# Attention with a Fourier-mixed FFN: the last block's fold in two parts, group 1's statistics and token sums later, the first streamed forms in h's place

## The chip, the cores and the metric

The kernel runs on one core of one Trainium2 chip. The metric is the device time of one execution in microseconds (us), as the median of several runs. The engines are TensorE (PE; PEld is its weight load), VectorE (DVE), ScalarE (ACT), GpSimd (POOL) and SyncE (SP), which issues nearly all DMAs.

## The reference

Attention over 4 batches, 8 heads, 768 tokens and head size 64, where a token sees 4 sink tokens and the 128 latest ones; then, over tokens (4, 768, 512), the real part of a two-dimensional FFT, a layer norm and a two-layer ReLU FFN:

```
x = attention(q, k, v)                         # (4, 768, 512)
u = x + real(fft(fft(x, axis=1), axis=2))
un = (u - mean(u)) / sqrt(var(u) + 1e-6)       # over the 512 channels
out = u + relu(un @ w_ch1) @ w_ch2             # 512 -> 2048 -> 512
```

All of it is float32. A product on PE is made of three: each factor is split in a high part that PE takes as it is and a low part (the rest), and hi·hi, hi·lo and lo·hi are added. So for each factor an engine casts the high part (ACT mostly) and another subtracts it (DVE or POOL).

## The kernel before

Tokens go in 24 blocks of 128, batches in the order 0, 2, 1, 3. Attention and the Fourier stage of the batch before it are interleaved in steps written out by hand; from step 97 on the tile scheduler orders the instructions of each engine by times of its own model and by pairs "this issues after that" (`issue_after`).

**Fourier stage of a batch.** `fold_n` (L355) adds and subtracts block j and block j + 3, `fold_m` (L362, L365) folds the 512 columns about their middle, `fold_hi` (L368, ACT) and `fold_lo` (L371, DVE) split the result into gh and gl. `stage1` (L398) multiplies by cosines and sines: za uses columns 0 to 255, zr column 256, zb the columns from 257 on. `stage2` gives a (L425) and b (L446), `combine` (L451, L452) their difference and sum d, `update` (L462, L463) adds d to u. The last batch to be folded is batch 3, whose third pair of blocks (j = 2) contains the last token block of attention. In the tail the updates of batch 2 run beside it.

**FFN.** The 24 blocks form six groups of four. Group 0 is computed directly: for each f = 0 to 15 (128 of the 2048 hidden units) `ch1` (L703, 12 matmuls, first layer), `split` (relu's high part on ACT L1192, low part on DVE L1193) and `ch2` (L1199, 12 matmuls, second layer) of the f before. Meanwhile the weights arrive as pairs of 32-bit words (raw) and are converted to float32 by `convert`: three DVE steps (L639 to L641), ACT's high part and POOL's low part, for the first layer into w_ring (L650, L651), for the second into w (L665, L666). W1's pairs of blocks are also combined for the later groups by `combine_w1` on POOL: four differences tq (L677 to L680), of which ACT and POOL make high and low parts `to` (L685, L686); SP stores w_ring and `to` in a DRAM tensor (L654, L687).

Groups 1 to 5 use seven products for each pair of halves in place of eight. The forms of W1 are streamed from that DRAM tensor into eight places (`load`, L1394, issued on SP) and used by `product` (L1421: 12 matmuls of 256 columns, PSUM banks pA, pB, pC). ACT and DVE put the products together, `halves` splits the relu into hring, and `unit` (L1449) is the second layer. The places are the buffers ld of the raw weights, `to`, tq and h. hring lies in the buffer of group 0's transposed tokens (un_slots), free after the last `ch1`. Tokens of the next group are prepared beside a group: statistics (L530 to L552), deviations, `make` (normalise), `turn` (transpose on PE into a PSUM bank, copied by ACT into xf, L1257), and sums of token halves (L1298, L1301) with their high (L1295) and low parts. For group 1 this is the generator `prepare_1`, of which three steps follow each f from 6 on.

Of the kernel before, what the change touches and what calls it, by code (L numbers as in the profile page):

```python
# [19 lines left out]
P = 128  # L20
# [42 lines left out]
F_LAST = (1, 1), (2, 2), (3, 3)  # L63
# [142 lines left out]
def kernel(  # L206
# [67 lines left out]
    def run(general):  # L274
        tag = "g" if general else ""
        with ExitStack() as p1:
# [59 lines left out]
            def fourier(b, at, ready):  # L336
# [20 lines left out]
                def fold_m(eng, j, odd):  # L357

                    g = t_["eo", j, 0]
                    if odd:  # L360
                        t = t_.pop(("eo", j, odd))
                        eng.tensor_tensor(g[:, 257:512], t[:, 1:256], t[:, 511:256:-1], op=ALU.subtract)  # L362
                        t_["g", j] = t_.pop(("eo", j, 0))
# [3 lines left out]
                def fold_hi(j):  # L367
                    A.copy(gh[:, j], t_["g", j])  # L368

                def fold_lo(j):  # L370
                    V.tensor_tensor(gl[:, j], t_.pop(("g", j)), f32(gh[:, j]), op=ALU.subtract)  # L371
# [97 lines left out]
                for j in range(NHALF):  # L469
# [3 lines left out]
                    f_n, f_m, f_s = F_LAST if tail and j == NHALF - 1 else (F_N, F_M, F_S)  # L473
# [153 lines left out]
            def convert(i, pool=None):  # L627
# [16 lines left out]
                if which == 0:  # L644
# [6 lines left out]
                    G.tensor_tensor(d[1], tf, f32(d[0]), op=ALU.subtract)  # L651
# [19 lines left out]
            def combine_w1(p, pool):  # L671

                t = state.pop(("t", p))
                b11, b21, b12, b22 = t[:, 0, :256], t[:, 0, 256:], t[:, 1, :256], t[:, 1, 256:]
# [516 lines left out]
            def split(h, x):  # L1191
                state["relu"] = A.activation(h[0], x, AF.Relu).ins  # L1192
                V.scalar_tensor_tensor(h[1], x, 0.0, f32(h[0]), op0=ALU.max, op1=ALU.subtract)  # L1193
# [144 lines left out]

            po = [ps_o.tile([P, DM], F32, tag=f"o{i}", name=f"o{i}_0") for i in range(len(groups[0]))]
            hs = {}  # L1340
            for i in (2, 3):
                convert(i, wa)
            for f in range(NF):
                ps = hp.pop(0) if f < 2 else ch1(0, f, unT0)
                hs[f] = g0.tile([P, 2, 512], F32R, tag="h", name=f"h_sb{f}", bufs=2)
                hs[f] = [hs[f][:, i] for i in range(2)]
                split(hs[f], ps)
                if pw is None:
# [21 lines left out]
                for _ in range(PREP_N if f >= PREP else 0):  # L1370
                    next(steps, None)
# [4 lines left out]
            for i in sorted(stores):  # L1376
                for fn in stores.pop(i):
                    fn()
# [3 lines left out]


            T_PLACE = {1: 0, 2: 1, 4: 2, 6: 3}
            stream = [(w_dram, it, W_PLACE[k]) for it in range(NIT) for k in range(7)]
            for g in range(2, len(groups)):
                stream += [(w_dram, i, W_PLACE[k]) for it in range(0, NIT, 2) for k in range(7) for i in (it, it + 1)]
                stream += [(t_dram, it, T_PLACE[k]) for k in (1, 2, 4) for it in range(NIT)]

            def load(n):  # L1390
                if n < len(stream):
                    d, it, k = stream[n]
                    for j in range(2):
                        nc.sync.dma_start(f32(places[n % NWS][:, j]).rearrange("p s c -> p (s c)"), d[2 * it + j][:, k])  # L1394

            w1_t = g0.tile([P, 2, 2, 2, 256], F32R, tag="to", name="w1_t")
            places += [w1_t[:, 0], w1_t[:, 1], g0.tile([P, 2, 2, 256], F32R, tag="tq", name="w1_q")]
            places.append(g0.tile([P, 2, 2, 256], F32R, tag="h", name="w1_h0", bufs=2))
            for n in range(NWS - 1):
                load(n)  # L1400
# [4 lines left out]
            with tc.manual_schedule():  # L1405
# [3 lines left out]
                hring = npool.tile([P, 4, 2, 2, 256], F32R, tag="un_slots", name="hring", bufs=1)  # L1409
# [4 lines left out]
                def product(n, k, ps):  # L1414
                    w = places[n % NWS]
# [8 lines left out]
                    load(n + NWS)  # L1424
# [75 lines left out]
                load(NWS - 1)  # L1500
# [292 lines left out]
```

## Time and profile before

| | |
|---|---|
| runs, us | 746.4, 746.86, 748.05; median 746.86 |
| the profiled execution | 747.63; span 745.9, so 1.73 around it |
| mean granted clock of PE | 0.994 |
| busy, us | PE 715.6, DVE 560.5, ACT 357.3, POOL 274.4 |
| first FFN group, end of the attention | about 210 to 326.7 us of the span |
| group 1 | 326.7 to 416.5 us |

Times in the timelines are from the start of the span. A timeline's row gives the start, the length of a run of like instructions, the engine, the line, what is written and read, the shape, the count, and in brackets how long the engine stood before it and what ended that. In the list of waits each row has the total, the number of waits and the longest.

### The profile page before, as it was taken

To read this page: it belongs to the slowest core of one execution; us is meant where nothing else is said; L and a number is where in the kernel's file an instruction comes from. 1 tells how busy PE (TensorE), PEld (TensorE's weight loads), DVE (VectorE), ACT (ScalarE), POOL (GpSimd) and SP (SyncE) were. 2 spreads that over 40 slices of the span, in tenths; PEclk is the share of its full clock that TensorE was granted. 3 is DMA by queue.
4 is the path that set the end of the run, shared out by engine and by line. 5 is a ranking of instruction groups with operands and counts; after the bars stand their busy time and mean duration, and the time that the engine had idled before them with its cause. 6 is when DMAs were issued, how large, how long until landed. Compare 5 with 4: busy or idle time off the path is not lost.

```text
span 745.9 us, 15695 instructions
## 1 busy us (share of the span) xinstructions
PE 715.6 (96%) x5539; PEld 642.6 (86%) x5539; DVE 560.5 (75%) x1299; ACT 357.3 (48%) x901; POOL 274.4 (37%) x391
## 2 busy tenths in 40 slices
PE   8999998989979999898999999999999999999996
PEld 6776876867868888687989999999999999999996
DVE  7778578888899988858668667947697578846773
ACT  5887666766634537313324134534444245523541
POOL 3567467577557989824994000000000000000000
PEclk9999999999999999999999999999999999999998
DMA  9863525533207999779999798979974897759721
GB/s 304 289 173 106 149 73 165 174 94 103 86 21 237 328 346 330 277 277 385 374 301 327 246 348 277 313 239 379 375 242 167 321 378 261 255 205 390 269 98 62
DMA packets 109576, 181.69 MB, mean 244 GB/s; under 512 B 9868, under 2 KB 44812, under 8 KB 108336
## 3 DMA queue, kind: packets, MB, share of 16 engines
q1 hardware_dynamic: 109200, 176.83, 69.6%
q0 software_dynamic: 288, 3.76, 1.3%
q8 instruction: 46, 0.75, 0.4%
q14 instruction: 42, 0.34, 0.1%
HBM read 148.04 MB, written 32.51 MB: 242 GB/s over the span
## 4 chain that ended last, share of the span: by engine, by line
PE 50%; DVE 4%; ACT 1%; issue 1%; SPq 0%; DMA 0%; POOL 0%; DVEq 0%
PE pB L1421 10%; PE qB L1598 9%; PE pA L1421 7%; PE pC L1421 6%; PE qC L1598 6%; PE qA L1598 6%; PE o L1449 5%; DVE bn L530 1%; PE unt L571 1%; DVE hring L1193 0%; DVE x L1657 0%; DVE x L1660 0%; SPq L1394 0%; DVE un L565 0%; DVE stat L531 0%
## 5 line engine op out<-in xcount | busy, mean ns | idle before, releaser
L1620 ACT CAST hring<-x 128x512 fp32r<-128x512 f32 x92 | 57.0, 619 | 52.0 <-PE qB L1598 19.6
L811 ACT ACTIVATE sm<-sm,mx 128x132 f32<-128x132 f32 x192 | 75.9, 400 | 4.6 <-DVE mx L805 4.6
L1624 DVE TENSOR_TENSOR hring<-x,hring 128x512 fp32r<-128x512 f32 x92 | 63.4, 689 | 14.8 <-ACT hring L1620 9.3
L786 PE MATMUL s<-ring,q 64*128 64x260 f32 x320 | 49.0, 411 | 5.9 <-DVE mx L805 2.7
L805 DVE CUSTOM_DVE_ANT_0 sm<-s,mask 128x132 f32<-128x132 f32 x192 | 48.5, 293 | 6.2 <-DVE s L792 0.9
L703 PE MATMUL h<-un_slots,w_ring 128*128 128x512 f32 x192 | 49.7, 405 | 3.4 <-POOL w_ring L651 2.9
L703 PEld LDWEIGHTS h<-un_slots,w_ring 128*128 128x128 f32 x192 | 36.3, 194 | 12.4 <-POOL w_ring L651 4.1
L786 PEld LDWEIGHTS s<-ring,q 64*128 64x128 f32 x320 | 26.9, 185 | 18.2 <-issue 5.0
L1598 PE MATMUL qA<-w,hring 128*128 128x256 f32 x312 | 39.8, 279 | 0.0
L1449 PE MATMUL o<-w,hring 128*128 128x512 f32 x156 | 38.5, 393 | 1.3 <-ACT hring L1192 1.1
L850 ACT COPY pta<-pt 128x512 f32<-128x512 f32 x48 | 28.1, 585 | 24.1 <-PE pt L843 24.0
L881 PE MATMUL xt<-ptl,ldv 128*64 128x128 f32 x384 | 39.3, 285 | 0.0
L1199 PE MATMUL o<-w,h_sb 128*128 128x512 f32 x156 | 38.1, 392 | 0.0
L1598 PEld LDWEIGHTS qA<-w,hring 128*128 128x128 f32 x312 | 37.9, 189 | 0.0
L811 ACT ACTIVATION_READ_ACCUMULATOR sm<-sm,mx 128x1 f32 x192 | 36.7, 191 | 0.0
L792 DVE COPY_PREDICATED s<-older,s 128x256 f32<-128x256 uint8 x80 | 33.7, 421 | 3.1 <-PE s L786 3.1
L859 POOL TENSOR_SCALAR_AFFINE_SELECT ptl<-pta 128x512 f32<-128x512 f32 x48 | 31.5, 655 | 11.6 <-ACT pta L850 11.6
L1598 PE MATMUL qB<-w_c,hring 128*128 128x256 f32 x288 | 35.2, 281 | 0.0
L1449 PEld LDWEIGHTS o<-w,hring 128*128 128x128 f32 x156 | 28.5, 188 | 7.5 <-ACT hring L1192 1.3
L881 PEld LDWEIGHTS xt<-ptl,ldv 128*64 128x64 f32 x384 | 22.1, 136 | 14.6 <-issue 4.8
L1598 PEld LDWEIGHTS qB<-w_c,hring 128*128 128x128 f32 x288 | 34.5, 189 | 0.0
L1199 PEld LDWEIGHTS o<-w,h_sb 128*128 128x128 f32 x156 | 29.1, 188 | 6.1
(296 smaller groups left out, 1965.3 us busy)
## 6 DMA issues: line engine op xcount, KB each, us to landing
w_c<-wd SPq DMA_DIRECT2D x96, 256.0 KB, 5.0
w_h<-wd SPq DMA_DIRECT2D x76, 256.0 KB, 5.1
w_t<-wd SPq DMA_DIRECT2D x70, 256.0 KB, 4.7
raw<-in_moe_w_ch_dram SPq DMA_DIRECT2D x32, 512.0 KB, 4.5
w_c<-td SPq DMA_DIRECT2D x48, 256.0 KB, 4.6
w_q<-wd SPq DMA_DIRECT2D x38, 256.0 KB, 5.0
wd<-to SPq DMA_DIRECT2D x8, 1024.0 KB, 6.4
ldv<-in_v_dram SPq DMA_DIRECT2D x28, 256.0 KB, 3.3
```

The lines of the kernel that those rows point to most:

```text
L703: T.matmul(ps[:, :tb], a[cc], x[:, :, cc, :], start=n == 0, stop=n == 3 * NCC - 1)
L786: T.matmul(ps[:, j, :P + W], st["q", g][rows, hp, :], keys(g, 2 * hp + j), start=True, stop=True)
L792: V.copy_predicated(ps[:, :, P + NS:P + W], older[qi > 2], ps[:, :, 0:P])
L805: V.tensor_tensor_reduce(sm[:, h % 4], ps[:, j, P:P + W], mask[min(qi, 3)], -SCALE, 3.0e38, ALU.add, ALU.min, accum_out=mx[:, 0, h:h + 1])
L811: A.activation(sm[:, h % 4], sm[:, h % 4], AF.Exp, bias=mx[:, 0, h:h + 1], scale=-1.0, accum_out=mx[:, 1, h:h + 1])
L881: T.matmul(ps[D * j:D * j + D, p, :], st["v", kb(g) - i][:, h, :], a[:, h % 4, :], start=i == 0, stop=i == n - 1)
L1199: T.matmul(po[i], a[:, P * i:P * i + P], x, start=f == 0 and n == 0, stop=f == NF - 1 and n == 2)
L1421: T.matmul(ps[:, 256 * j:256 * j + 256], w[:, j, a, cs], x[:, xs], start=BANK.index(BANK[k]) == k and j == c == m == 0, stop=j == c == 1 a ...
L1449: T.matmul(po[i], h[:, a, j, ts_], x, start=first and j == m == 0, stop=last and j == 1 and m == 2)
L1598: T.matmul(ps[:, 256 * t:256 * t + 256], h[:, a, j, P * t:P * t + P], x, start=BANK.index(BANK[k]) == k and c == t == j == m == 0, stop=c ...
L1620: A.copy(hi, x)
L1624: V.tensor_tensor(*args, op=ALU.subtract)
```

## The change

- **Fold.** The last block pair of batch 3 is folded in two column parts, 0 to 256 and 257 to 511: one fold sum, its column fold, high and low part for the first, then the same for the second. The late updates of batch 2 begin two steps later, h of f = 1 comes at place 14 and not 10, and the conversions of the second-layer weights 0 and 1 move behind the relu of f = 0.
- **Group 1's preparation.** The number of steps behind each f is a table, and each step issues after the relu's parts of that f. Statistics start behind f = 6, the token sums behind f = 13.
- **`combine_w1`.** Two differences of 256 columns become one instruction, issued after the low part of the pair's second weight.
- **Streamed forms.** The first four forms go to hring, their loads issued behind `ch1` of f = 15; the next three follow, and then the stores that were left, then four more loads. The order of the places changes with that.
- **Group 2's preparation** beside group 1's products: the statistics begin at step 3 and not 0, and the transposes use the PSUM banks in another order.

```
-F_LAST = (1, 1), (2, 2), (3, 3)
+F_TAIL = (1, 1), (2, 2), (3, 3)
-UPD_LATE = 36
+UPD_LATE = 38
-CONV_AT, CH1_AT = (3, 5), (9, 10)
+CONV_AT, CH1_AT = (3, 5), (9, 14)
-PREP_N = 3
+PREP_N = {6: 3, 7: 3, 8: 2, 9: 2, 10: 2, 11: 1, 13: 2, 14: 2, 15: 3}
...
+                    if tail and j == NHALF - 1:
+                        for i, cs in enumerate((slice(0, 257), slice(257, DM))):
+                            at(k + 1 + i, "V", lambda i=i, j=j: fold_n(V, j, i))
+                            at(k + 1 + i, "V", lambda i=i, j=j: fold_m(V, j, i))
+                            at(k + 2 + i, "A", lambda j=j, cs=cs: fold_hi(j, cs))
+                            at(k + 2 + i, 0, lambda j=j, cs=cs: fold_lo(j, cs))
+                        continue
...
-                    G.tensor_tensor(d[1], tf, f32(d[0]), op=ALU.subtract)
+                    state["lo", f] = G.tensor_tensor(d[1], tf, f32(d[0]), op=ALU.subtract).ins
...
-                G.tensor_tensor(q[:, 1], b12, b11, op=ALU.subtract)
+                with tc.issue_after(state["lo", 2 * p + 1]) if p else ExitStack():
+                    G.tensor_tensor(q[:, 1:3], t[:, 1].rearrange("p (h c) -> p h c", h=2), t[:, :, :256], op=ALU.subtract)
-                G.tensor_tensor(q[:, 2], b22, b12, op=ALU.subtract)
...
-            for i in (2, 3):
-                convert(i, wa)
             for f in range(NF):
                 ps = hp.pop(0) if f < 2 else ch1(0, f, unT0)
+                if f == NF - 1:
+                    hring = npool.tile([P, 4, 2, 2, 256], F32R, tag="un_slots", name="hring", bufs=1)
+                    for n in range(NH):
+                        load(n)
...
+                for i in (2, 3) if f == 0 else ():
+                    convert(i, wa)
...
-                for _ in range(PREP_N if f >= PREP else 0):
-                    next(steps, None)
+                for _ in range(PREP_N.get(f, 0)):
+                    with tc.issue_after(state["h_lo"]), tc.issue_after(state["relu"]):
+                        next(steps, None)
...
-                todo = {0: [(statistics, 0)], 1: [(statistics, 1, 2)], 2: [(statistics, 3)], 3: [(deviate, 7)], 5: [(deviate,), (make, 0)],
+                todo = {3: [(statistics, 0)], 4: [(statistics, 1)], 6: [(statistics, 2)], 7: [(statistics, 3)], 8: [(deviate, 1)],
...
```

On DVE, the kernel before has this at the end of attention, from the last block's addition (us_5) to the relu of f = 0; f_3_2 is the folded last pair, gl its low part, cw and cv conversions, d and u batch 2:

```order
L909 TENSOR_TENSOR us_5_2607<-x_3138,mx_2693 128x512
L362 TENSOR_TENSOR f_3_1_3127<-f_3_1_3129 128x255
L355 TENSOR_TENSOR f_3_2_3152<-us_2_2604,us_5_2607 128x512
L355 TENSOR_TENSOR f_3_2_3154<-us_2_2604,us_5_2607 128x512
L451 TENSOR_TENSOR d_1_3177<-asb_1_3149,b_2_3156 128x257
L452 TENSOR_TENSOR d_1_3177<-asb_1_3149,b_2_3156 128x257
L365 TENSOR_TENSOR f_3_2_3152<-f_3_2_3152 128x255
L371 TENSOR_TENSOR gl_2995<-f_3_1_3127,gh_2994 128x512
L362 TENSOR_TENSOR f_3_2_3152<-f_3_2_3154 128x255
L462 TENSOR_TENSOR u_65<-u_65,d_2_3123 128x257
L463 TENSOR_TENSOR u_65<-u_65,d_2_3123 128x255
L640 SCALAR_TENSOR_TENSOR cw_3246<-raw_2987,cw_3246 128x512
```

Behind these come the low part of the whole last pair (L371), a conversion step (L641) and the relu's low part (L1193). In the changed kernel the same place of DVE reads (line numbers from here on are those of the changed kernel, a line or some more apart):

```order
L917 TENSOR_TENSOR us_5_2607<-x_3142,mx_2693 128x512
L370 TENSOR_TENSOR gl_2995<-f_3_1_3100,gh_2994 128x512
L380 TENSOR_TENSOR sph<-xr_3008,sph 1x257
L355 TENSOR_TENSOR f_3_2_3154<-us_2_2604,us_5_2607 128x512
L450 TENSOR_TENSOR d_1_3178<-asb_1_3152,b_2_3157 128x257
L364 TENSOR_TENSOR f_3_2_3154<-f_3_2_3154 128x255
L451 TENSOR_TENSOR d_1_3178<-asb_1_3152,b_2_3157 128x257
L355 TENSOR_TENSOR f_3_2_3181<-us_2_2604,us_5_2607 128x512
L370 TENSOR_TENSOR gl_2995<-f_3_2_3154,gh_2994 128x257
L362 TENSOR_TENSOR f_3_2_3154<-f_3_2_3181 128x255
L1201 SCALAR_TENSOR_TENSOR h_sb_3232<-h_0_3164,h_sb_3232 128x512
L370 TENSOR_TENSOR gl_2995<-f_3_2_3154,gh_2994 128x255
```

The first part's low piece is now the ninth row from us_5 and the relu's low part the eleventh; the update of batch 2 and the conversion steps stand behind both parts.

On POOL, the kernel before has this for the last two pairs of f (w_ring: low parts of the first layer, w_1: of the second, tq: differences, to: their low parts):

```order
L651 TENSOR_TENSOR w_ring<-tw_4007,w_ring 128x2x256
L677 TENSOR_TENSOR tq_4090<-tw_4007 128x256
L679 TENSOR_TENSOR tq_4090<-tw_4007 128x256
L678 TENSOR_TENSOR tq_4090<-tw_4007,tq_4090 128x256
L651 TENSOR_TENSOR w_ring<-tw_4007,w_ring 128x2x256
L680 TENSOR_TENSOR tq_4090<-tw_4007,tq_4090 128x256
L666 TENSOR_TENSOR w_1_4075<-cv_4067,w_0_4074 128x512
L666 TENSOR_TENSOR w_1_4087<-cv_4078,w_0_4086 128x512
L686 TENSOR_TENSOR to_4091<-tq_4090,to_4091 128x2x256 x2
L651 TENSOR_TENSOR w_ring<-tw_4131,w_ring 128x2x256
```

and the changed kernel this:

```order
L694 TENSOR_TENSOR to_3953<-tq_3952,to_3953 128x2x256
L658 TENSOR_TENSOR w_ring<-tw_3994,w_ring 128x2x256
L694 TENSOR_TENSOR to_3953<-tq_3952,to_3953 128x2x256
L658 TENSOR_TENSOR w_ring<-tw_3994,w_ring 128x2x256
L686 TENSOR_TENSOR tq_4076<-tw_3994 128x512
L687 TENSOR_TENSOR tq_4076<-tw_3994,tq_4076 128x256
L688 TENSOR_TENSOR tq_4076<-tw_3994,tq_4076 128x256
L673 TENSOR_TENSOR w_1_4061<-cv_4053,w_0_4060 128x512
L673 TENSOR_TENSOR w_1_4073<-cv_4064,w_0_4072 128x512
L658 TENSOR_TENSOR w_ring<-tw_4115,w_ring 128x2x256
L694 TENSOR_TENSOR to_4077<-tq_4076,to_4077 128x2x256 x2
L658 TENSOR_TENSOR w_ring<-tw_4115,w_ring 128x2x256
```

The three difference instructions now follow both low parts of w_ring of their pair, and a low part of the next pair stands ahead of the two `to`.

## Rows read from the trace of the kernel before

**Rows 1.** The page: the span, and each engine's busy time.

```profile
span 745.9 us, 15695 instructions
PE 715.6 (96%) x5539; PEld 642.6 (86%) x5539; DVE 560.5 (75%) x1299; ACT 357.3 (48%) x901; POOL 274.4 (37%) x391
```

**Rows 2.** PE's waits over the whole run: the waiting instruction <- what ended the wait, then total us, count, longest.

```profile
PE h L703 <- POOL w_ring L651: 2.9, 2, 1.5
...
PE pB L1421 <- DMA w_c<-wd: 1.3, 1, 1.3
PE o L1449 <- ACT hring L1192: 1.1, 1, 1.1
...
PE pB L1421 <- ACT xf L1257: 1.0, 1, 1.0
...
PE o L1449 <- DVE hring L1193: 0.2, 1, 0.2
```

**Rows 3.** Stretches: from:to and length, then busy us and instructions of PE, PEld, DVE, ACT and POOL, PE's granted clock, the DMA engines' mean share, GB/s.

```profile
215.00:222.00 7.00, 3.42 (x18) 2.47 (x18) 7.00 (x13) 1.71 (x4) 3.69 (x4) 1.00 0.00 0
222.00:226.00 4.00, 4.00 (x11) 3.13 (x12) 4.00 (x8) 0.91 (x2) 2.31 (x2) 0.57 0.60 154
...
222.00:240.00 18.00, 18.00 (x81) 15.87 (x82) 17.23 (x30) 7.18 (x14) 13.60 (x13) 0.91 0.74 249
...
304.00:326.70 22.70, 19.84 (x86) 15.60 (x85) 13.95 (x22) 7.38 (x13) 18.01 (x17) 1.00 0.79 297
326.70:350.00 23.30, 19.76 (x138) 17.71 (x137) 17.43 (x34) 6.57 (x13) 3.81 (x5) 1.00 1.02 366
350.00:416.50 66.50, 66.50 (x409) 59.30 (x408) 48.30 (x54) 22.18 (x38) 48.71 (x44) 1.00 0.96 319
```

**Rows 4.** Timeline of PE in the tail: b of batch 2, the za sum of batch 3, h of f = 1, h of f = 2.

```profile
216.07 0.95 PE L446 MATMUL b<-cst,zb 128*128 128x258 f32 x6 [1.05 <-DVE d L452]
...
218.98 0.62 PE L398 MATMUL za<-cst,gh 128*128 128x386 f32 x2 [0.91 <-ACT gh L368]
220.64 0.44 PE L398 MATMUL za<-cst,gl 128*128 128x386 f32 x1 [1.04 <-DVE gl L371]
...
221.84 4.60 PE L703 MATMUL h<-un_slots,w_ring 128*128 128x512 f32 x12 [0.59 <-DVE h_sb L1193]
...
235.73 2.88 PE L703 MATMUL h<-un_slots,w_ring 128*128 128x512 f32 x12
```

**Rows 5.** Timeline of DVE in the same stretch, and as the last row ACT's high part of the last pair.

```profile
211.13 0.75 DVE L381 TENSOR_TENSOR sph<-xr,sph 1x257 fp32r<-1x257 f32 x1
211.91 0.69 DVE L909 TENSOR_TENSOR us<-x,mx 128x512 f32<-128x512 f32 x1
...
212.85 2.41 DVE L355 TENSOR_TENSOR f<-us,us 128x512 f32<-128x512 f32 x2
215.18 0.41 DVE L451 TENSOR_TENSOR d<-asb,b 128x257 f32<-128x257 f32 x1
...
216.18 1.22 DVE L371 TENSOR_TENSOR gl<-f,gh 128x512 fp32r<-128x512 f32 x1
...
219.91 0.68 DVE L371 TENSOR_TENSOR gl<-f,gh 128x512 fp32r<-128x512 f32 x1
...
221.11 0.68 DVE L1193 SCALAR_TENSOR_TENSOR h_sb<-h,h_sb 128x512 fp32r<-128x512 f32 x1
...
227.38 0.68 DVE L641 SCALAR_TENSOR_TENSOR tw<-raw,cw 128x512 int32<-128x512 int32 x1
...
218.31 0.62 ACT L368 CAST gh<-f 128x512 fp32r<-128x512 f32 x1 [1.90 <-DVE f L362]
```

**Rows 6.** Timeline of PE at the end of the first group and the start of the streamed one: h of f = 14 and of f = 15 (10 of 12 matmuls each), the second layer of the last two f, the second product.

```profile
305.95 2.56 PE L703 MATMUL h<-un_slots,w_ring 128*128 128x512 f32 x10 [1.36 <-POOL w_ring L651]
...
313.23 2.56 PE L703 MATMUL h<-un_slots,w_ring 128*128 128x512 f32 x10 [1.49 <-POOL w_ring L651]
...
321.16 5.67 PE L1199 MATMUL o<-w,h_sb 128*128 128x512 f32 x24
...
329.55 1.69 PE L1421 MATMUL pB<-x,w_c 128*128 128x256 f32 x12 [1.30 <-DMA w_c<-wd]
```

**Rows 7.** Timeline of POOL: the low part for f = 2; the one for f = 14; the two low parts of `to`.

```profile
230.17 1.29 POOL L651 TENSOR_TENSOR w_ring<-tw,w_ring 128x512 fp32r<-128x512 f32 x1
...
304.62 1.28 POOL L651 TENSOR_TENSOR w_ring<-tw,w_ring 128x512 fp32r<-128x512 f32 x1
...
309.37 2.57 POOL L686 TENSOR_TENSOR to<-tq,to 128x512 fp32r<-128x512 f32 x2
```

**Rows 8.** Groups of POOL's instructions from 200 to 330 us: total busy us, mean ns of one | idle time before them.

```profile
L651 POOL TENSOR_TENSOR w_ring<-tw,w_ring 128x512 fp32r<-128x512 f32 x16 | 21.5, 1346 | 0.0
...
L677 POOL TENSOR_TENSOR tq<-tw 128x256 f32<-128x256 f32 x8 | 6.4, 806 | 5.9 <-DVE tw L641 3.6 <-issue 1.2 <-DVE stat L542 1.0
```

**Rows 9.** SP's queue: four loads behind the last store. Then the streamed forms w_c from 318 to 345 us: lengths of their issues (min, median, max in ns), and us from issue to landing. Last, ACT's square root of group 2's statistics.

```profile
324.30 2.97 SPq L1394 DMA_DIRECT2D w_c<-wd  x4
...
L1394 SPq DMA_DIRECT2D w_c<-wd x12: 319/395/1703, 317.0 to 340.4; - x12
...
DMA to landing us min/median/max: 3.4/5.2/6.5
...
335.82 0.21 ACT L540 ACTIVATE stat<-stat 128x4 f32<-128x4 f32 x1 [2.44 <-DVE stat L537]
```

More of the change, by code (lines that the diff above doesn't have):

```diff
@@ L1337, in do, with place, load @@
                     s += 1
+            T_PLACE = {1: 0, 2: 1, 4: 2, 6: 3}
+            stream = [(w_dram, it, W_PLACE[k]) for it in range(NIT) for k in range(7)]
+            for g in range(2, len(groups)):
+                stream += [(w_dram, i, W_PLACE[k]) for it in range(0, NIT, 2) for k in range(7) for i in (it, it + 1)]
+                stream += [(t_dram, it, T_PLACE[k]) for k in (1, 2, 4) for it in range(NIT)]
+            NH = 4
+            def place(n):
+                return hring[:, n] if n < NH else places[(n - NH) % NWS]
+            def load(n):
+                if n < len(stream):
+                    d, it, k = stream[n]
+                    for j in range(2):
+                        state["load"] = nc.sync.dma_start(f32(place(n)[:, j]).rearrange("p s c -> p (s c)"), d[2 * it + j][:, k]).ins
             po = [ps_o.tile([P, DM], F32, tag=f"o{i}", name=f"o{i}_0") for i in range(len(groups[0]))]
             hs = {}
-            for i in (2, 3):
-                convert(i, wa)
             for f in range(NF):
                 ps = hp.pop(0) if f < 2 else ch1(0, f, unT0)
+                if f == NF - 1:
+                    hring = npool.tile([P, 4, 2, 2, 256], F32R, tag="un_slots", name="hring", bufs=1)
+                    for n in range(NH):
+                        load(n)
                 hs[f] = g0.tile([P, 2, 512], F32R, tag="h", name=f"h_sb{f}", bufs=2)
@@ L1375, in run @@
                 late.pop()()
+            places = [npool.tile([P, 2, 2, 256], F32R, tag="ld", name=f"w1_c{i}", bufs=LDB) for i in range(LDB)]
+            with tc.issue_after(state["load"]):
+                for n in range(NH, NH + LDB):
+                    load(n)
             for i in sorted(stores):
-                for fn in stores.pop(i):
-                    fn()
-            places = [npool.tile([P, 2, 2, 256], F32R, tag="ld", name=f"w1_c{i}", bufs=LDB) for i in range(LDB)]
[L1384 to L1394, printed above, removed]
+                with tc.issue_after(state["load"]) if i > 2 * NF else ExitStack():
+                    for fn in stores.pop(i):
+                        fn()
             w1_t = g0.tile([P, 2, 2, 2, 256], F32R, tag="to", name="w1_t")
-            places += [w1_t[:, 0], w1_t[:, 1], g0.tile([P, 2, 2, 256], F32R, tag="tq", name="w1_q")]
+            places += [g0.tile([P, 2, 2, 256], F32R, tag="tq", name="w1_q"), w1_t[:, 0], w1_t[:, 1]]
             places.append(g0.tile([P, 2, 2, 256], F32R, tag="h", name="w1_h0", bufs=2))
-            for n in range(NWS - 1):
-                load(n)
+            with tc.issue_after(state["load"]):
+                for n in range(NH + LDB, NH + NWS - 1):
+                    load(n)
             ch2(NF - 1, hs.pop(NF - 1), po)
@@ L1414, in product @@
                 def product(n, k, ps):
-                    w = places[n % NWS]
+                    w = place(n)
                     xh, xl = (t[:, k] for t in state["x"])
@@ L1423, in product @@
                                          skip_group_check=True)
-                    load(n + NWS)
+                    if n >= NH:
+                        load(n + NWS)
                 po, units = {}, []
@@ L1593, in product2 @@
                             if k in (1, 2, 4):
-                                w = [places[n % NWS][:, j, a] for a in range(2)]
+                                w = [place(n)[:, j, a] for a in range(2)]
                             else:
```

25 lines of the change are left out of this document (12 added, 13 removed).

## The prediction

> **What bounds the kernel now.** I read the page's totals first: TensorE (PE) is busy 715.6 of 745.9 us, and no other engine is near that [rows 1]. A change can therefore gain little more than the idle time of PE, plus time lost to a lower clock, so the second view is the list of what ended PE's waits [rows 2]. Five of its entries lie where the change works: 2.9 us behind GpSimd's (POOL's) low parts of the first-layer weights, 1.3 behind a transfer of a streamed form, 1.1 and 1.0 behind ScalarE (ACT), 0.2 behind VectorE (DVE). The table by stretches then says where PE loses time [rows 3]: in 215 to 222 us it is busy 3.42 of 7, in 304 to 326.7 only 19.84 of 22.7, in 326.7 to 350 only 19.76 of 23.3; from 350 to 416.5 it has no gap. In 222 to 226 it has none either, but the granted clock there is 0.57: part of it ran at the lower level, 1.2 GHz, after PE had been busy only half of the stretch before. The timelines of the three stretches give the single waits [rows 4 to 7].
>
> **The fold of the last block (the tail, 204 to 236 us).** PE has four waits here: 1.05 for the pair of `combine`, 0.91 for the high part gh, 1.04 for the low part gl, 0.59 for the low part of the relu, h_sb [rows 4], 3.59 together. All hang on one queue, DVE's: the last gl, which PE's za sum needs, ends at 219.91 + 0.68 = 220.59, because the second half of the fold, an update of batch 2 and a step of a weight conversion stand ahead of it. In the new order DVE comes to the low part of columns 0 to 256, the only ones that the two za sums read, soon after the fold sums. Counted from the addition us_5 (it ended at 212.60 with the row step sph ahead of it, so near 212 with sph behind), the new queue to that point is: gl of block 1, 0.68 to 1.22; sph, 0.75; two whole fold sums of 128x512, the pair 2.41 in this row and at least 1.2 if a piece takes no longer than us_5; three half pieces at 0.41; the gl piece of 257 columns, 0.41 like the 257-column subtraction [rows 5]. That is 0.68 + 0.75 + 1.2 + 1.23 + 0.41 = 4.3 at least and 1.22 + 0.75 + 2.41 + 1.23 + 0.41 = 6.0 at most: 216.3 to 218.0, against 220.59. PE's h of f = 1 also waits for the relu's low part of f = 0 (it started at 221.84, as that ended), which stands two pieces behind, 0.41 + 0.68: 217.4 to 219.1, in the middle 218.2. That is 3.6 sooner, all of the four waits; I count 3.3, between 2.7 and 3.59.
>
> The split adds one gl piece and one cast: two pieces at 0.41 for one at 0.68 is 0.14 on DVE, and on ACT two short casts for one of 0.62 [rows 5], between nothing and 0.6 more; both lie beside PE's h of f = 0 and come into the time only through the queue just counted.
>
> The slow h: its 12 matmuls took 4.60 us where the same 12 took 2.88 later [rows 4]. With PE nearly gapless from 211 on I expect the clock to stay at 2.4 GHz: another 1.7. Bounds: 0 if it falls all the same, 1.72 if not.
>
> What is late next: the conversions of the second-layer weights for f = 0 and 1 now stand behind the relu of f = 0, and PE comes to f = 2 some five microseconds sooner, at about 230.7 for 235.73 [rows 4]. From the new gl piece (near 217) to the end of the conversion for f = 2 DVE has 17 steps, some 9.6 us at 0.41 to 0.68 each [rows 5]: near 226.7. Before, 3.4 us passed from there (227.38 + 0.68) to the end of POOL's low part (230.17 + 1.29) [rows 5, 7], which makes 230.1. That is half a microsecond of slack: I take 0.2 off. The tail gives 3.3 + 1.7 - 0.2 = 4.8, between 2.7 and 5.3.
>
> **A rule that speaks against the pieces.** One low part took 1.22 us and the other, of the same shape, 0.68 [rows 5]: something beside the first one held it up by 0.54. The Trainium skill, SBUF — State Buffer, section "Who interferes with whom", says that a VectorE instruction with two inputs in SBUF contends with a GpSimd instruction that reads SBUF, and that the shared ports are held for the whole instruction while the other is blocked. Taken at its word, the piece more is one more chance to stand behind POOL, and by a whole low part of POOL, 1.3, the tail would give 3.5 and not 4.8; the row agrees in kind, with 0.54.
>
> **The first FFN group, f = 2 to 15.** PE waits for POOL's low part at f = 14 (1.36) and f = 15 (1.49) [rows 6], 2.85 in all. On POOL the low part for f = 14 (at 304.62) stands behind differences of the same pair, the one for f = 15 behind two low parts of the forms to be stored (2.57 us from 309.37) [rows 7]. The change puts the difference steps (tq) behind the low part of the pair's second weight, so the first wait loses its cause by order; the second loses part of it, since one of the two pieces of `to` now stands behind the weight. The token sums on DVE, which delayed the conversions, go behind the 14th block. The merged subtraction makes one instruction of 512 columns, about 1.35, of two of 0.81 [rows 8]: 0.3 per pair on POOL, nothing on PE directly. The statistics leave 136 to 138 us and 238 to 255 us, where PE has no waits: zero for that, but it gives DVE slack.
>
> Against it: per pair of f POOL has six low parts at about 1.35 (two each of w_ring, of w and of `to`, priced alike) and four differences at 0.81 [rows 8], 11.3 us, some 11.0 after the merge; PE needs twice the 5.5 us that 24 matmuls take from 321.16 to the group's end at 326.7 [rows 3, 6], 11.0 too. POOL keeps pace but cannot catch up, and PE arrives 4.8 sooner. New places to stand: the second-layer weight of f = 15 now queues behind 2.57 us of `to`, and the last relu on ACT behind a cast or two of 0.6. Between minus 1 (both late) and 2.85 (both waits gone) I take 1.9: one wait goes by order, 1.36, and a third of the other.
>
> **The start of the streamed group.** PE's waits: 1.3 for the second form's transfer, 1.1 + 0.2 for the relu, 1.0 for the PSUM bank that ACT copies out of [rows 2], 3.6 in all. Transfer: stores stand between the loads on SyncE's (SP's) queue, and the four loads after the last store are issued from 324.30 on, 2.4 us ahead of PE, while landing takes 3.4 to 6.5 us [rows 9]. Now eight loads go out directly behind the last matmul of h of f = 15, and PE still has 24 matmuls, 5.5 us, before the first product. That needs two issues of about 0.4 and a landing of 5.2 [rows 9], 5.6 from the second issue: 0.1 late, and each next form is wanted up to 1.69 us later [rows 6]. I keep 0.3 for a stand (0 to 2, if issues are as slow as the 2.97 us for four). Relu: it stood behind a square root that itself waited 2.44 us for DVE [rows 9]; the statistics of group 2 now begin three steps later, so this goes, but casts of 0.6 come ahead of the relu, 0.2 kept. Bank: the transposed tokens now use the other bank first, so 1.0 goes, 0.2 kept for its mirror at a later step. 3.6 - 0.7 = 2.9, between 1 and 3.6.
>
> **Sum.** 4.8 + 1.9 + 2.9 = 9.6. The profiled execution took 747.63 (span 745.9 and 1.73 around it), so 738.0 for it; the median of the runs, 746.86, lies 0.77 below, so I predict 737.3. All waits and the clock together, 3.59 + 1.72 + 2.85 + 3.6 = 11.8, make the lower end: 735.1, and 734.9 with some scatter of the runs.
>
> **Rivals.**
> The pace of POOL and DVE in the first group eats what the tail gives: PE then stands at f = 2, or at 13 to 15, for 4.8 in total, and the gain is 1.9 + 2.9 = 4.8, a time of 742.1. For it: 11.0 against 11.0 above. Against: POOL was busy 18.01 of the last 22.7 us of the group and 13.60 of 18 at its beginning [rows 3], so there is room of some 4 us at either end.
> The clock falls again in the tail: 1.7 less, 739.0. For it: a gap of a microsecond can stay, since the sooner end of the range above comes after PE's own work. Against: the half-idle stretch before the fall, 215 to 222, goes.
> The change doesn't do what it says: the pieces stand in the new order, but their start is set by us_5 and by POOL beside them, and the two `to` pieces keep POOL as late as before; only the streamed group gains, 2.9: 744.0. For it: the fold pair took 2.41 us, twice the lower bound, while PE was ahead. Against: the new gl piece has less ahead of it under any durations of the rows.
> Slower: POOL works in order, and the differences now wait for the low part of the second weight; if that pushes `to` and the next pair's low parts back each time, PE stands at every f from 2 on as it did at 14 and 15, 1.43 us on average. That decides beyond (4.8 + 2.9) / 1.43 = 5.4 stands more than the two of before; with 14 it is 20.0 against 7.7 + 2.85, 9.5 slower: 756.4. Against: PE waited at two of 14, and POOL's order puts the weights first now.
>
> **How the numbers follow.** Forecast 0.62; the clock 0.10; pace 0.18; not what it says 0.06; slower 0.04. The forecast's own range, by the bounds of its terms, is 734.9 to 740.5; most of the pace case lies under 742.5, so 734.9 to 742.5 leaves out about 0.2. A measurement of this kernel can tell 0.2%, 1.5 us, from no change. Faster by more: forecast, clock, and the other two but for their worst ends, 0.91; within: those ends, 0.05; slower: 0.04.
>
> **What would show it.** In the changed kernel's list of PE's waits the entries for gl, gh, `combine` and w_ring are gone or under 0.3 each; PE's h of f = 1 starts near 218.2 and takes 2.8 to 2.9; f = 2 starts near 231; the first product of the streamed group starts near 320 with no wait over 0.3 for hring, and PE is busy throughout the first 14 products. I am wrong if h of f = 1 starts after 220, if the granted clock falls in the tail, if a wait over 1 us for w_ring or for a second-layer weight stands anywhere in f = 2 to 15, or if the first product stands for its transfer over 1 us.

## The result and the profile after

The changed kernel takes 752.2 us in the median of ten runs, against 746.9 for the kernel before: a ratio of 1.0066, with a 95% interval of 1.0049 to 1.0082. It was forecast 9.6 us faster and is some 5 us slower. The profiled execution spans 750.3 us, 4.4 more than before, and no engine's busy time differs by more than 6 us from [rows 1] (the page of the changed kernel):

```profile
span 750.3 us, 15677 instructions
...
PE 719.1 (96%) x5539; PEld 646.5 (86%) x5539; DVE 566.5 (76%) x1300; ACT 357.2 (48%) x902; POOL 271.6 (36%) x383
```

A total like this says nothing of the place. PE runs its work in nearly the same order in all kernels of this study, so its timeline can be cut at five starts, and the stretches between them compared. The starts of the changed kernel (timeline of PE; line numbers are those of each kernel):

```profile
210.47 0.86 PE L711 MATMUL h<-un_slots,w_ring 128*128 128x512 f32 x3
...
231.46 2.88 PE L711 MATMUL h<-un_slots,w_ring 128*128 128x512 f32 x12
...
324.88 1.58 PE L1442 MATMUL pA<-x,hring 128*128 128x256 f32 x12
...
411.68 8.40 PE L1471 MATMUL o<-w,hring 128*128 128x512 f32 x36
```

These are h of f = 0, h of f = 2, the first product of the streamed group, and group 1's last stretch of the second layer. For the kernel before, h of f = 2 starts at 235.73 [rows 4], and the other three are:

```profile
210.56 0.40 PE L703 MATMUL h<-un_slots,w_ring 128*128 128x512 f32 x1
...
326.67 1.58 PE L1421 MATMUL pA<-x,w_c 128*128 128x256 f32 x12
...
408.28 8.41 PE L1449 MATMUL o<-w,hring 128*128 128x512 f32 x36
```

| stretch, us | before | changed | difference | forecast |
|---|---|---|---|---|
| attention, to h of f = 0 | 210.56 | 210.47 | -0.1 | 0 |
| tail, to h of f = 2 | 25.17 | 20.99 | -4.2 | -4.8 |
| first group, to the first product | 90.94 | 93.42 | +2.5 | -1.9 |
| group 1, to its last second layer | 81.61 | 86.80 | +5.2 | -2.9 |
| the rest | 337.62 | 338.62 | +1.0 | 0 |

So the tail did what was forecast, and both later stretches went the other way. PE's waits in the changed kernel:

```profile
PE pA L1442 <- ACT tmp L1556: 3.6, 1, 3.6
PE unt L578 <- DVE un L572: 2.5, 3, 1.7
...
PE o L1207 <- POOL w L673: 1.6, 2, 0.9
...
PE unt L578 <- ACT un L570: 1.6, 1, 1.6
PE b L445 <- DVE d L451: 1.3, 1, 1.3
...
PE pC L1442 <- DVE tmp L1574: 0.6, 1, 0.6
```

None of the five entries of [rows 2] that the forecast counted on is there any more; others stand in their place. PE's granted clock tells of a second cost (stretches, columns as in [rows 3]):

```profile
215.00:222.00 7.00, 5.60 (x30) 4.98 (x31) 7.00 (x15) 2.29 (x5) 3.20 (x4) 1.00 0.06 7
222.00:226.00 4.00, 4.00 (x23) 3.83 (x22) 3.89 (x7) 2.88 (x6) 2.38 (x3) 1.00 0.67 178
272.00:283.00 11.00, 9.31 (x36) 7.04 (x35) 10.65 (x19) 7.36 (x14) 6.97 (x7) 0.84 0.76 271
330.00:341.00 11.00, 8.07 (x35) 7.53 (x36) 6.47 (x12) 2.94 (x5) 0.00 (x0) 0.69 0.93 331
```

In the tail the clock no longer falls. It falls behind the new wait at f = 9 and behind the one of 3.65 us at the fourth product. The timeline of PE gives what each wait costs and what the lower clock adds:

```profile
272.78 3.34 PE L1207 MATMUL o<-w,h_sb 128*128 128x512 f32 x12
277.69 1.11 PE L578 MATMUL unt<-ident,un 128*128 128x128 f32 x4 [1.56 <-ACT un L570]
278.45 4.21 PE L711 MATMUL h<-un_slots,w_ring 128*128 128x512 f32 x12
...
319.66 3.23 PE L1207 MATMUL o<-w,h_sb 128*128 128x512 f32 x12 [0.69 <-POOL w L673]
323.84 1.21 PE L1207 MATMUL o<-w,h_sb 128*128 128x512 f32 x4 [0.94 <-POOL w L673]
...
332.93 2.93 PE L1442 MATMUL pA<-x,hring 128*128 128x256 f32 x12 [3.65 <-ACT tmp L1556]
335.66 2.76 PE L1442 MATMUL pB<-x,w_c 128*128 128x256 f32 x12
338.22 3.34 PE L1471 MATMUL o<-w,hring 128*128 128x512 f32 x12
...
354.45 0.63 PE L578 MATMUL unt<-ident,un 128*128 128x128 f32 x4 [1.69 <-DVE un L572]
```

The first group: 2.85 of waits [rows 6] went; 1.56 + 0.69 + 0.94 = 3.19 came; the slow transposes and the slow h add 1.7 (1.11 for 0.60, 4.21 for 3.00 at full clock). The second layer before them adds 0.4 (3.34 for 2.93), but not by the clock, which was 1.00 from 272.7 to 276.2 us: its weight load stood 0.55 us for POOL's low part of a second-layer weight. That is +2.5 of the +2.5. Counted from h of f = 0, the two waits of [rows 6] and [rows 7] that are put at f = 14 and 15 lie in h of f = 13 and 14; h of f = 15 started at 318.39 and waited for nothing. Group 1: 3.5 of waits went; 3.65 + 1.69 + 0.59 = 5.93 came; two products at 2.93 and 2.76 for 1.57 and a second layer at 3.34 for 2.92 add 3.0. That is +5.4 of the +5.2.

Where the 3.65 come from is seen on ACT and on SP's queue. ACT's first copy out of the product's bank did nothing for 10.54 us, and what ended that was a store:

```profile
332.29 0.59 ACT L1556 COPY tmp<-pA 128x512 f32<-128x512 f32 x1 [10.54 <-DMA wd<-w_ring]
```

```profile
317.15 3.65 SPq L1363 DMA_DIRECT2D hring<-wd  x8
320.89 4.57 SPq L1363 DMA_DIRECT2D w_c<-wd  x6
325.83 0.32 SPq L661 DMA_DIRECT2D wd<-w_ring  x1
```

The change moved the last store of w_ring behind 14 loads; in the kernel before it was issued ahead of all of them:

```profile
316.55 0.33 SPq L654 DMA_DIRECT2D wd<-w_ring  x1
```

It reads the buffer tagged "ring", and `tmp`, into which ACT copies, is the next tile with that tag. The program lets nothing be written there until the store has landed: 6.4 us after its issue, and the copy started 6.5 us after it.

### The profile page after: what moved, and what is told of

Its sections match the earlier page's. It is cut to its first block, busy times and chain, and to the rows that moved or that the text cites. A ratio compares the mean times of both kernels' runs of the same rounds, so it can differ in the third digit from the quotient of the medians.

```text
span 750.3 us, 15677 instructions
## 1 busy us (share of the span) xinstructions
PE 719.1 (96%) x5539; PEld 646.5 (86%) x5539; DVE 566.5 (76%) x1300; ACT 357.2 (48%) x902; POOL 271.6 (36%) x383
## 4 chain that ended last, share of the span: by engine, by line
PE 70%; DVE 13%; POOL 6%; DMA 4%; ACT 3%; issue 3%; SPq 1%; POOLq 0%; ACTq 0%; DVEq 0%
PE pB L1442 9%; PE qB L1621 9%; PE pA L1442 7%; PE pC L1442 6%; PE qA L1621 6%; PE qC L1621 6%; PE o L1471 4%; PE xt L889 4%; PE s L794 4%; PE h L711 3%; PE o L1207 2%; PE pt L851 2%; PE za L397 1%; PE unt L578 1%; DVE sm L813 1%
## 5 line engine op out<-in xcount | busy, mean ns | idle before, releaser
L1442 PE MATMUL pB<-x,w_c 128*128 128x256 f32 x348 | 45.7, 285 | 0.0
L1442 PEld LDWEIGHTS pB<-x,w_c 128*128 128x128 f32 x348 | 43.7, 193 | 0.0
```

Source lines behind the costliest of these rows:

```text
L1442: T.matmul(ps[:, 256 * j:256 * j + 256], w[:, j, a, cs], x[:, xs], start=BANK.index(BANK[k]) == k and j == c == m == 0, stop=j == c == 1 a ...
```

## The experiments

All are the kernels before or changed with few edits. The same stretches can be read for each (the attention before h of f = 0 is the same work in all and ended between 210.06 and 212.85 in the profiles, mostly because PE waited 0 to 2.4 us for loads of v or of q and k, so stretches compare better than whole times). The stretches are those of one profiled execution each, the ratio is from all runs. In e8 nothing is moved but DMAs late in the first group, and that stretch is 1.1 shorter than in the kernel before; differences of a microsecond between two stretches are therefore not shown by them alone.

| kernel | ratio to before, 95% | tail | first group | group 1 | rest |
|---|---|---|---|---|---|
| e1 | 1.0025, 1.0009 to 1.0040 | 21.01 | 92.02 | 83.62 | 338.60 |
| e2 | 0.9993, 0.9981 to 1.0006 | 20.95 | 89.76 | 84.61 | 338.73 |
| e3 | 1.0005, 0.9987 to 1.0023 | 21.01 | 90.78 | 83.55 | 338.72 |
| e4 | 1.0069, 1.0052 to 1.0086 | 20.93 | 94.41 | 85.38 | 338.02 |
| e5 | 0.9990, 0.9973 to 1.0008 | 21.00 | 92.03 | 80.60 | 338.90 |
| e6 | 0.9974, 0.9958 to 0.9990 | 20.94 | 90.94 | 83.46 | 338.35 |
| e7 | 1.0076, 1.0052 to 1.0101 | 24.92 | 91.83 | 82.89 | 338.27 |
| e8 | 1.0078, 1.0050 to 1.0106 | 25.17 | 89.82 | 86.60 | 337.16 |
| e9 | 0.9975, 0.9962 to 0.9989 | 20.99 | 90.82 | 82.48 | 339.11 |
| e10 | 1.0037, 1.0024 to 1.0050 | 20.97 | 95.16 | 81.65 | 338.05 |

**e1, the store ahead of the loads.**

```
                 if f == NF - 1:
                     hring = npool.tile([P, 4, 2, 2, 256], F32R, tag="un_slots", name="hring", bufs=1)
+                    for fn in stores.pop(2 * NF + 2, ()):
+                        fn()
                     for n in range(NH):
```

> The changed kernel, with one DMA moved: the last store of w_ring is issued ahead of the loads of the first streamed forms and not behind seven of them. Theory (the store holds a buffer): ScalarE's first copy of the streamed group writes tmp, which lies in w_ring's buffer, and it waited 10.54 us until the late store (issued at 325.83) had landed; PE stood 3.65 us behind it at the fourth product and then ran 2.96 us longer at the lower clock. So the copy should start near 326.4, both losses go, and the time falls by 6.6, from 752.2 to about 745.6. Rival (the loads are what is late, the store only ends last): the store ahead delays the loads by its own transfer, PE stands at the first product for 1 to 3 us, and the gain is under 3 us, 749 or more.

The copy starts at 326.94 and waits for no store; PE's wait of 3.65 and the lower clock behind it are gone, and the four products read from hring run without a gap. The theory on the store holds, the rival falls: no product waits for its form. But group 1 became 3.2 shorter and not 6.6: the next wait grew from 1.69 to 3.00, the clock fell behind it (0.61 from 352 to 355 us; two products took 2.19 and 2.60 for 1.66 and 1.58, 1.6 more), and the wait of pC grew from 0.59 to 1.05. Copy, store, and the rows of that next wait, of e1 (ACT; SP; PE; DVE; POOL):

```profile
326.94 0.59 ACT L1558 COPY tmp<-pA 128x512 f32<-128x512 f32 x1 [4.78 <-issue]
...
314.69 0.33 SPq L661 DMA_DIRECT2D wd<-w_ring  x1
...
349.73 0.63 PE L578 MATMUL unt<-ident,un 128*128 128x128 f32 x4 [3.00 <-DVE un L572]
...
345.41 1.22 DVE L555 SCALAR_TENSOR_TENSOR stat<-stat 128x4 f32<-128x4 f32 x1
346.66 1.18 DVE L557 TENSOR_TENSOR stat<-stat 128x4 f32<-128x4 f32 x1
...
349.05 0.54 DVE L572 TENSOR_SCALAR un<-u,stat 128x512 f32<-128x512 f32 x1
...
345.31 2.52 POOL L1506 TENSOR_TENSOR tmp<-tmp 128x512 fp32r<-128x512 f32 x2 [3.84 <-ACT tmp L1505]
```

PE comes to the transposes of group 2's first tokens (step 12) before they are normalised: the change moved the end of their statistics from step 5 to 10 and the normalising of the first tokens from 5 to 11, but the first transpose only from 7 to 12.

**e2, the statistics of group 1 free to go early** (e1, and the steps behind f = 6 to 8 without `issue_after`):

```
                 for _ in range(PREP_N.get(f, 0)):
+                    if f < 9:
+                        next(steps, None)
+                        continue
                     with tc.issue_after(state["h_lo"]), tc.issue_after(state["relu"]):
                         next(steps, None)
```

> As e1, and the statistics and first token steps of group 1 (those behind f = 6 to 8) are no longer held behind the relu's parts, so the scheduler may put them earlier, as in the kernel before; the later steps are held as in the changed kernel. Theory (the held statistics come too late): VectorE's chain of statistics ran from 267 to 277 us and PE stood 1.56 us for the normalised tokens at f = 9 and lost some 2.2 us at the lower clock behind it; both go, 3.8 below e1, about 741.8. Rival (VectorE has no room for them before f = 6, since PE comes 4.3 us sooner): PE waits for weights at f = 2 to 8 instead, and the time is that of e1 or above it.

The 1.57 at f = 9 are gone, and the first group is 2.3 shorter than in e1: the theory is right in kind. It is short of 3.8 because e1's own profile had no lower clock there to lose, because 0.4 of the 2.2 was a second-layer weight and not the clock, and because the wait for that weight, just ahead of the transposes, grew:

```profile
276.53 1.20 PE L1207 MATMUL o<-w,h_sb 128*128 128x512 f32 x4 [1.26 <-POOL w L673]
```

Group 1 is 1.0 longer than in e1, and the ratio, 0.9993, is 0.3% below e1's (some 2.4 us), not the 3.8 us of the theory.

**e3, POOL's order at the end of the first group** (e1, and the last pair's `to` behind the low part of the last second-layer weight):

```
-                        G.tensor_tensor(o[:, j:j + 2, 1], q[:, j:j + 2], f32(o[:, j:j + 2, 0]), op=ALU.subtract)
+                        with tc.issue_after(state["w_lo"]) if p == NPR - 1 else ExitStack():
+                            G.tensor_tensor(o[:, j:j + 2, 1], q[:, j:j + 2], f32(o[:, j:j + 2, 0]), op=ALU.subtract)
```

> As e1, and on POOL the low parts of the last pair's streamed forms (to) issue behind the low part of the last second-layer weight. Theory (POOL's order): PE's second wait for w, 0.94 us at f = 15, goes; the first, 0.69 for the weight of f = 14, stays, since the differences stand ahead of that one. 0.9 below e1, about 744.7. Rival (VectorE's conversion is the late part, so the order on POOL gives nothing): the time of e1; or the later store of to makes the loads behind it late and a wait for a form appears in the first 14 products.

As the theory had it: the second wait for w is gone, the first (0.7) stays, and the first group is 1.2 shorter than e1's, with no new wait for a form. The ratios of e1 and e3 (1.0025, 1.0005) have overlapping intervals, so the whole time alone doesn't show it.

**e4, the fold alone** (the kernel before with the first bullet of the change).

> The kernel before with only the fold's part of the change (two column parts, updates two steps later, h of f = 1 and the conversions 2 and 3 later). Theory (what the tail gives is kept, at least in part): f = 2 starts near 231.5 and not 235.7 as in the changed kernel, and PE's waits for w_ring grow by at most 2 us: 742.6 to 744.6. Rival (POOL and VectorE set the pace of the first group): the gain of 4.3 at f = 2 is given back by f = 15 through waits for weights, and the time stays within 1.5 us of 746.9.

Neither. The tail gives its 4.2, and then the two later stretches lose more than that between them: 3.5 and 3.8. PE's waits of e4 from 260 to 350 us, and its SP queue where the loads of the streamed forms begin:

```profile
PE pB L1428 <- DMA w_c<-wd: 3.8, 1, 3.8
PE h L710 <- POOL w_ring L658: 2.9, 2, 1.5
PE o L1206 <- POOL w L673: 0.9, 1, 0.9
```

```profile
325.16 0.32 SPq L694 DMA_DIRECT2D wd<-to  x1
325.58 2.94 SPq L1401 DMA_DIRECT2D w_c<-wd  x4
```

PE is earlier, but POOL's last `to` and its store are not (325.16; 323.88 in the kernel before), and the loads queue behind that store. A wait of 1.30 [rows 6] has become 3.82, and after it and after the first wait for w_ring, at f = 12, the granted clock fell (0.71 in 326 to 334 us, 0.72 in 296 to 302). That is why a part that is 4.2 faster by itself makes the whole slower, not merely equal.

**e5, the transposes of group 2 later** (e1, and):

```
-                        12: [(turn, 0, *banks[0][:2]), (make, 1)], 14: [(turn, 1, *banks[0][:2]), (make, 2)],
+                        14: [(turn, 0, *banks[0][:2]), (make, 1)], 17: [(turn, 1, *banks[0][:2]), (make, 2)],
```

> As e1 (store ahead of the loads), with the first two transposes of group 2's tokens two and three steps later (14 and 17 in place of 12 and 14). Theory (the transposes come before their tokens): in e1 PE stood 3.0 us at step 12 for the normalised tokens, because the later statistics ended only at 348.5 on VectorE, and ran some 1.6 us longer at the lower clock behind it; at step 14 PE comes 5.6 us later and finds them, so both go: the stretch from the first product to group 1's last second layer takes 79.5 to 80 in place of 83.6, and the time is some 4 us under e1, about 744. Rival (VectorE is the bound of this stretch, not the order): the wait moves to the next VectorE result, as it did when the store's wait was taken away (pC behind tmp, 0.6 to 1.05), and the stretch stays above 82.

The 3.00 and the wait of pC behind it are gone, the clock stays up, and group 1 takes 80.60, 1.0 less than in the kernel before. The theory holds; two waits for the relu (0.48 and 1.19) are what came instead, so it ends 0.6 above the expected 79.5 to 80. The ratio moved by 0.35% against e1, some 2.6 us and not 4.

**e6, all three mends together** (e1, e2, e3, e5).

> As e5, with the statistics free to go early (e2) and the last second-layer weight ahead of the streamed forms on POOL (e3). Theory (the three late steps were the whole loss): 20.95 for the tail, at most 89.8 for the first group (e2's value, with the second wait at f = 15 gone if it is there), 80 for group 1's stretch: 5.0 under the kernel before by these stretches, less 1.0 that all kernels of this change lose after it: about 742. Rival (the conversions on VectorE and POOL set the end of the first group): the first product starts no earlier than in e2 counted from f = 2, and the whole stays above 744.

Ratio 0.9974: faster than the kernel before, the interval clear of 1, but by 2 us and not 5. Both numbers of the rival came: the first group took 90.94, longer than e2's, and the whole stayed above 744. With every known wait taken out PE stood 2.0 us for second-layer weights; in group 1, 2.9 longer than in e5, it stood 2.2 for a relu that ACT had queued behind a cast waiting for POOL, and ran slower behind that. The gains of the parts don't add.

**e7, all but the fold** (e1 with the fold's part undone).

> As e1, but the fold, its updates, the place of h of f = 1 and of the conversions 2 and 3 as in the kernel before. Theory (PE's earlier arrival is kept once the loads no longer hang on POOL's last streamed forms): the tail takes 25.2 again and the group the 92.0 of e1 or less, so it is 2 to 4 us slower than e1, 750 to 752. Rival (the conversions end at the same time whether PE comes early or not): the first group shortens by what the tail loses, to 88 to 89, and the time is that of e1 within 1 us.

The theory: 24.92 and 91.83, and the ratio is 0.5% (3.8 us) above e1's. With the other parts in place, most of what the fold gives is kept.

**e8, the late store alone**, in the kernel before:

```
             for n in range(NWS - 1):
                 load(n)
+                if n == LDB:
+                    with tc.issue_after(state["load"]):
+                        for fn in stores.pop(2 * NF + 2):
+                            fn()
```

> The kernel before with one edit: the last store of w_ring issues behind the loads of the fourth or fifth streamed form and not ahead of all loads. Theory (the store holds tmp's buffer): the store lands after 332, ScalarE's first copy of the streamed group waits for it, PE stands 2 us or more at the fourth product and then runs at the lower clock: 3 to 7 us slower, 749.5 to 753.5. Rival (such a wait is hidden behind the loads that are late anyway): within 1.5 us of 746.5.

As the theory had it: 0.78% slower by this edit alone, group 1 5.0 longer. The store goes out at 330.78, the copy starts 6.0 later, PE waits 5.16 and then runs slower (SP, ACT, PE of e8):

```profile
330.78 0.43 SPq L654 DMA_DIRECT2D wd<-w_ring  x1
...
336.78 0.58 ACT L1537 COPY tmp<-pA 128x512 f32<-128x512 f32 x1 [13.59 <-DMA w_t<-wd]
...
337.42 2.89 PE L1425 MATMUL pA<-x,w_t 128*128 128x256 f32 x12 [5.16 <-ACT tmp L1537]
```

The view names a load as the releaser here, not the store. The copy's place, and e1, where moving the store alone removed the wait, say which it is; a name in brackets is inferred from the last event.

**e9, the transposes of group 1 later, too** (e5 and e3, and):

```
-PREP_N = {6: 3, 7: 3, 8: 2, 9: 2, 10: 2, 11: 1, 13: 2, 14: 2, 15: 3}
+PREP_N = {6: 3, 7: 3, 9: 2, 10: 2, 11: 2, 12: 1, 13: 2, 14: 2, 15: 3}
```

> As e5 with the last second-layer weight ahead of the streamed forms on POOL (e3), and the transposes of group 1's tokens one f later (table 6: 3, 7: 3, 9: 2, 10: 2, 11: 2, 12: 1, then as in the changed kernel); the statistics stay behind f = 6. Theory (group 1's transposes, too, come before their tokens, and nothing but their place need move): PE's 1.57 for the tokens at f = 9 goes without the new wait for a second-layer weight that the early statistics of e2 and e6 brought, and the 0.95 at f = 15 goes as in e3; the first group takes 89 to 89.5 and group 1's stretch e5's 80.6, together with the tail's 21.0 some 7 us under the kernel before, less 1 behind group 1: ratio 0.991 to 0.995. Rival (VectorE and POOL set the pace; each wait removed comes back at the next weight): the first group stays at 90.8 or more, ratio 0.997 to 1.0.

Here the rival is right. The wait for tokens is gone, those for second-layer weights are down to 0.2 each, and the first group still takes 90.82: a low part of w_ring that POOL makes late (0.95), and small waits on ACT. Group 1 took 82.48 and not e5's 80.6, with 1.22, 1.19 and 0.65 of waits for the relu. Ratio 0.9975, as e6.

**e10, fold and streamed forms alone** (the kernel before with these two parts, the store ahead of the loads).

> The kernel before with two parts of the change alone: the fold in two parts, and the first four streamed forms in hring, with the last store of w_ring ahead of the loads (preparation of both groups and the differences on POOL as before). Theory (in e4 the fold's gain was lost where the loads hang on POOL's last streamed forms, whose time PE's earlier arrival does not change): the wait of 3.82 for a form and the lower clock behind it go, the three waits for weights of e4 stay; 20.9, 94.4 and 80 to 81 for the three stretches, 1 to 2.5 us under the kernel before, ratio 0.9965 to 0.9985. Rival (the conversions' end sets the streamed group's start whatever the loads' place): the wait comes back at the first products for a transfer or for a token sum, and the time stays near e4's, ratio 1.004 or more.

The wait of 3.82 is gone, and group 1 takes before's 81.6. But the first group takes 95.16, 4.2 more than before: just what the tail gave. PE's waits from 290 to 320 us, and its first product:

```profile
PE h L710 <- POOL w_ring L658: 4.4, 3, 1.6
```

```profile
326.30 1.58 PE L1442 MATMUL pA<-x,hring 128*128 128x256 f32 x12
```

It starts at 326.30; 326.67 in the kernel before. PE came to f = 2 4.6 us sooner than there and is 0.4 sooner at the end of the group; in e4 it was 4.7 and 1.3. So with preparation and POOL's order as before, the weights that POOL makes late take back most of what PE gains. The ratio, 1.0037, is outside the theory's range; the rival's 1.004 was nearer, though not by the waits that it named. The profiled execution is the fastest of e10's six, and its stretches add up to before's within 0.5: where the other runs lose their 1.4 to 2.5 us against it, no trace shows.

## Why the prediction was wrong, by its steps

**The fold: right.** In the new queue of DVE, the low piece that PE needs ended at 216.83 + 0.86 = 217.69 (forecast 216.3 to 218.0), the relu's low part at 218.63 (217.4 to 219.1), and h of f = 1 started at 218.84 (218.2):

```profile
216.83 0.86 DVE L370 TENSOR_TENSOR gl<-f,gh 128x257 fp32r<-128x257 f32 x1
...
217.95 0.68 DVE L1201 SCALAR_TENSOR_TENSOR h_sb<-h,h_sb 128x512 fp32r<-128x512 f32 x1
```

The clock stayed at 1.00 with PE busy 5.60 of 7 us ahead of the stretch. Of the four waits only that for `combine` stayed (1.26, and 1.05 before); the lower clock, 1.72, went as counted, and the tail gave 4.2 of 4.8. The wait for f = 2 that was feared did not come.

**The streamed forms: the failed step is "Now eight loads go out directly behind the last matmul", in which only the loads were priced.** Those were on time: PE stood for none of the forms. The two stores moved behind them were given no cost, and no work was named that hides one: what waits for the store of w_ring is the next writer of its buffer, `tmp`. Cost 3.65 and the lower clock, 3.0 (rows above; e1 takes it away, e8 puts it on the kernel before alone).

**Group 2's preparation: a wait without a term.** The wait for the bank went, and "0.2 kept for its mirror at a later step" did not come. What came at the same transposes is another wait, for the normalised tokens, which the forecast put at nothing: 1.69, and 3.00 in e1. The forecast saw the statistics leave the relu's way, but not that PE's transpose, 12 steps in, now came before a chain of DVE that ends late. e5 moves the transposes and the loss is gone.

**The first group: two steps failed.** "The statistics leave 136 to 138 us and 238 to 255 us, where PE has no waits: zero for that" priced the place they left and not the one they came to. They ran from 267 to 277 us on DVE, with a table load of ACT before the square root, and PE's transposes at f = 9 waited for them (DVE's first and ACT's last step, of the changed kernel):

```profile
266.98 0.68 DVE L537 BATCH_NORM_STATS2 bn<-u 128x6 f32<-128x512 f32 x1
...
275.61 1.21 DVE L559 SCALAR_TENSOR_TENSOR stat<-stat 128x4 f32<-128x4 f32 x1
...
271.19 1.28 ACT L547 ACT_TABLE_LOAD   x1
...
276.91 0.72 ACT L570 ACTIVATE un<-un,stat 128x512 f32<-128x512 f32 x1 [0.50 <-DVE stat L559]
```

And of the "new places to stand" one came: the second-layer weight of f = 15 stood behind `to` (0.94), that of f = 14 behind the differences (0.69); e3 removes the first of these. The prediction calls the waits for w_ring those of f = 14 and 15; they are those of 13 and 14, one weight earlier, and its reading of POOL's order holds for these. Both went, 2.85, where 1.9 was counted; the losses beside them were not.

**The rivals.** The pace of POOL and DVE, given 0.18, is the truest of them: e10 comes nearest to it (the first group gives back the tail's 4.2), e9 and e6 show it in part, and the 11.0 against 11.0 was its reason. As worked out it gave 742.1, since it counted waits alone; a new wait can also bring the lower clock. The rival for slower had another mechanism: PE was to stand at every f, and it stood at three places of the group.

**The signs and the range.** None of the four signs of being wrong came: h of f = 1 started at 218.84, the clock in the tail was 1.00, the longest wait for a second-layer weight was 0.94, and the first product did not stand. They watched the places that the forecast had priced, and the losses came where it had no price. The lower bounds of the three terms, 2.7 - 1 + 1 = 2.7, give 744.2, not the 740.5 that is called the forecast's own range.

**What stays open.** The rest, behind group 1, is 1.0 longer in the changed kernel and 0.4 to 1.5 in the experiments with its places, though PE's waits there are the same 0.9 us in both kernels: the starts there drift by steps of a tenth or so. e4 (0.4) and e8 (-0.5), with the old places, scatter by nearly as much; no run told the two apart.

## What to carry to other kernels

A DMA that is moved has two ends. For a store, look up which tile takes its buffer next and who writes that first, and price the store's issue and landing against it, as one would for a load. When a producer is moved later, move its consumer by as much, or show that the consumer has the slack; and before counting what an earlier engine gives, ask for each later hand-over (a load behind a store, a weight behind a conversion) whether its time follows that engine at all.

## What was not expected of the hardware

Steps on 128x4 elements that took 0.17 us in the kernel before took 1.2 when POOL worked beside them: the two of e1 above (345.41 and 346.66) lie on POOL's two instructions from 345.31 to 347.83, 1.26 each. The kernel before, at the same step, with POOL idle (DVE):

```profile
336.28 0.17 DVE L548 SCALAR_TENSOR_TENSOR stat<-stat 128x4 f32<-128x4 f32 x1
336.48 0.17 DVE L550 TENSOR_TENSOR stat<-stat 128x4 f32<-128x4 f32 x1
```

The same two steps took 1.18 to 1.22 us beside POOL in e2, e3, e5, e6 and e9, too, and 0.17 in e10, with POOL idle. In e1 they add 2.1 us to a chain that PE waited 3.00 us for; that the wait would be 0.9 without them is an estimate, as no run took POOL away from there.

The Trainium skill, SBUF — State Buffer, section "Who interferes with whom", says of a VectorE instruction with two inputs in SBUF beside a GpSimd one that reads SBUF that whoever comes second is blocked for the whole instruction of the other; the trace agrees here with 1.2 for 0.17. The forecast had weighed that rule on the long pieces of the fold, where it costs half an instruction, and not on the short steps of a chain, where it multiplies them by seven.

The same wait need not bring the same clock: at f = 9 PE stood 1.56 or 1.57 us in the changed kernel, e1, e3 and e5, and the h behind it took 4.21 us in the first and 2.98 to 3.00 in the other three, one execution each.
